# Chunked attention, Fourier mixing and an MLP on one core: the first batch's Fourier stage in halves, key blocks on partitions 32 to 127, and zero products in the planned gaps of TensorE

## The chip, the cores and the metric

The kernel runs on one core of a Trainium2 chip. The metric is the device time of one execution in microseconds (us). The engines are TensorE (PE; PEld is its weight load), VectorE (DVE), ScalarE (ACT), GpSimd (POOL) and SyncE (SP, which here only issues transfers).

## The reference

q, k and v are 4 batches x 8 heads x 768 positions x 64. Positions go in chunks of 32. Each chunk attends to 8 memory keys, the 16 positions before it, its own 32 and the 8 after it, with a softmax. The result, as x of 768 x 512 for each batch, goes through a two-dimensional Fourier transform of which the real part is kept, a norm, and an MLP of 512 to 2048 to 512:

```
X = fft(fft(x, axis=1), axis=2)
u = x + real(X)
un = (u - mean(u)) / sqrt(var(u) + 1e-6)
out = u + max(un @ w_ch1, 0) @ w_ch2
```

## The kernel before

**Planner.** `Plan` (L37 to L110) holds tasks: an engine, a cost in us, a function that emits the instructions, the tasks it comes after, the buffers it takes and gives (`take`, `give`) and a rank. `order` (L56) plays the time forward: whenever an engine is free in the plan, the first task by rank whose inputs are done and whose buffers are free is placed. What it emits is the fixed order of each engine's instructions; on the chip an engine never passes a waiting instruction. Loads count as `moved` us on one shared wire plus a lag of 2.0. PE costs count double before 40 us (L89).

**Attention** (L567 to L597) works on 16 pairs of heads, four for each batch, in the order 0, 2, 1, 3. Pair n: SP issues q, k (L256) and v in seven pieces (L275 to L281). Both are cast to bf16 (L262; on DVE for the first batch, on POOL for the others). PE turns them (`trq` L289, `trk` L305), ACT copies them out as `qT` (L294) and as key blocks `kTb` (L315), and DVE puts the memory keys in (L310). A key block is 96 rows: memory 0 to 7, then 88 positions. For each half g of the positions PE makes the scores `sc` (L326, 12 products), ACT the exponentials `e` (L334, two instructions), PE the values `xa` (L350, 24 products), and DVE divides by the sum into `xsb` (L360, L361), which is called the norm below. The first batch's `xa` uses two buffers in turn (tags xa, mlp).

**Fourier stage** (L646 to L706), per batch: DVE folds the channels (`zy` L374), then the sequence (`pq` L381, L382), then the channels again (`ff` L390, L391), for par 0 and 1. Each fold is split into two fp16 parts, `hi` on ACT (L399) and `lo` on DVE (L404). PE multiplies by the sequence tables (`ps` L414: 12 products for each of four parts, and 12 more for a single row). ACT and DVE copy the result out in two parts (`up` L426, L430) and DVE reverses it (`dn` L435). Then six blocks kt of columns follow: PE `pm` (L446), DVE sum and statistics (L452, L458, L459), ACT `un` (L464); the first batch's blocks are turned by PE (`tp` L471) and copied by DVE (`unT` L481), the others' by a transfer (L476). The sine tables are made on ACT after the first batch's last exponential (L617 to L622, L634). The weights are loaded through POOL's queue from the same point on (L640, L642).

**MLP** (L710 to L737), per batch in two halves of three blocks: 16 x 4 products `ph` (L497), ReLU on ACT to `hT` (L504, one buffer), 3 x 16 products `pc` (L511), DVE `osb` (L517) and the store (L521). Its tasks have the rank MLPS + number, so they are placed wherever nothing else is ready: they fill. This holds for the ReLU on ACT too:

```
def RELU(i):
    return MLPS + i
```

## Time and profile before

| | us |
|---|---|
| median of 3 runs (337.01 to 339.83) | 337.48 |
| the profiled execution's own time | 336.54 |
| its span | 334.8 |
| PE busy, of the span | 289.2 (86%) |
| DVE busy | 177.3 (53%) |
| ACT busy | 164.6 (49%) |
| POOL busy | 48.9 (15%) |
| PE `ph` L497, 512 products | 92.1 |
| PE `pc` L511, 384 products | 85.8 |
| chain that ended last: share of PE, DVE, ACT, DMA | 68%, 16%, 7%, 4% |

How to read it: 1.7 us of the execution's time lie outside the span. In a timeline each row is start, length, engine, line, operation, destination<-sources and count; square brackets give the engine's idle time before it and what ended that. The granted clock (PEclk) is 1.00 at 2.4 GHz and 0.50 at 1.2 GHz. The rows below read 1.00 up to 57 us as well, where the products take about twice as long as later.

### The profile page before, as it was taken

How to read it: one execution, taken by the hardware profiler on the slowest of the kernel's cores; microseconds unless marked ns; L12 is line 12 of the kernel's file. 1: busy time of each engine (PE TensorE's matmuls, PEld its weight loads, DVE VectorE, ACT ScalarE, POOL GpSimd, SP SyncE). 2: the span in 40 equal slices, each digit the busy share in tenths (PEclk: the TensorE clock that was granted, in tenths of full speed). 3: DMA queues.
4: the chain of work that ended last, by engine and by line, in shares of the span. 5: the costliest groups of instructions: out<-in, count | busy, mean ns of one | idle time of the engine just before them, and what ended most of it. 6: DMA issues, size and time to landing. Idle time of an engine off the chain costs nothing.

```text
span 334.8 us, 6729 instructions
## 1 busy us (share of the span) xinstructions
PE 289.2 (86%) x2761; PEld 187.1 (56%) x2761; DVE 177.3 (53%) x341; ACT 164.6 (49%) x290; POOL 48.9 (15%) x66
## 2 busy tenths in 40 slices
PE   0585847798999997978999996889999999999995
PEld 0464746676666674656745654655455454554542
DVE  5944169988599894998923369790110200101001
ACT  1364488556796546758525623246345062250620
POOL 8201471013333024320001000000010000000000
PEclk9999999899999999979999999799999999999999
DMA  8999899994999196980054200100420100101001
GB/s 168 208 217 197 180 226 205 198 216 118 206 184 162 55 224 129 232 139 3 2 113 117 29 2 2 40 23 33 108 80 2 63 32 31 65 2 63 31 33 63
DMA packets 60287, 35.18 MB, mean 105 GB/s; under 512 B 48480, under 2 KB 50528, under 8 KB 60256
## 3 DMA queue, kind: packets, MB, share of 16 engines
q1 hardware_dynamic: 53824, 24.19, 38.8%
q0 software_dynamic: 2688, 4.19, 6.9%
q10 hardware_dynamic: 3744, 6.36, 5.1%
q8 instruction: 22, 0.36, 0.5%
q14 instruction: 9, 0.07, 0.1%
HBM read 30.28 MB, written 6.29 MB: 109 GB/s over the span
## 4 chain that ended last, share of the span: by engine, by line
PE 68%; DVE 16%; ACT 7%; DMA 4%; issue 1%; SPq 1%; POOL 0%; ACTq 0%; POOLq 0%; DVEq 0%
PE pc L511 24%; PE ph L497 22%; PE xa L350 7%; PE ps L414 6%; PE pm L446 4%; ACT e L334 3%; PE sc L326 2%; DVE ff L391 2%; DVE lo L404 2%; DVE zy L374 2%; DMA mkf<-in_mem_k_dram 1%; DMA qf<-in_q_dram 1%; DMA unT<-un 1%; DVE xsb L361 1%; DVE pq L381 1%
## 5 line engine op out<-in xcount | busy, mean ns | idle before, releaser
L497 PE MATMUL ph<-unT,w_sb 128*128 128x384 f16 x512 | 92.1, 326 | 1.7 <-ACT hT L504 1.2
L504 ACT ACTIVATE hT<-ph 128x384 f16<-128x384 f32 x128 | 60.9, 490 | 65.2 <-PE ph L497 65.1
L511 PE MATMUL pc<-w_sb,hT 128*128 128x512 f16 x384 | 85.8, 379 | 0.0
L517 DVE SCALAR_TENSOR_TENSOR osb<-pc,rstd,xsb 128x512 f32<-128x512 f32 x24 | 18.0, 749 | 101.7 <-PE pc L511 101.7
L497 PEld LDWEIGHTS <-w_sb 128*128 128x128 f16 x512 | 48.1, 97 | 35.1 <-issue 6.2
L511 PEld LDWEIGHTS <-hT 128*128 128x128 f16 x384 | 37.2, 98 | 42.6 <-issue 0.3
L334 ACT ACTIVATE e<-sc,mbias 96x384 f32<-96x384 f32 x64 | 33.4, 571 | 22.2 <-PE sc L326 21.5
L350 PE MATMUL xa<-va,e 96*64 96x65 f32 x768 | 35.3, 252 | 10.2 <-ACT e L334 9.4
L350 PEld LDWEIGHTS xa<-va,e 96*64 96x64 f32 x768 | 30.4, 162 | 17.4 <-ACT e L334 10.4
L464 ACT ACTIVATE un<-xsb,mu_s 128x512 f16<-128x512 f32 x24 | 17.3, 720 | 29.1 <-DVE mu_s L459 9.1
L262 POOL CAST qb<-qf 96x1024 bf16<-96x1024 f32 x12 | 14.2, 1184 | 82.1 <-DMA qf<-in_q_dram 82.1
L360 DVE RECIPROCAL zs<-xa 128x6 f32<-128x6 f32 x32 | 6.1, 192 | 31.2 <-PE xa L350 31.1
L414 PE MATMUL ps<-cosS,hi 128*128 128x193 f16 (+1 forms) x72 | 16.6, 282 | 4.8 <-DVE ff L391 3.2
L414 PE MATMUL ps<-cosS,lo 128*128 128x193 f16 (+1 forms) x72 | 16.4, 282 | 4.8 <-DVE lo L404 4.8
L326 PE MATMUL sc<-qT,kTb 64*96 64x64 bf16 x384 | 16.9, 228 | 3.8 <-ACT kTb L315 2.0
L426 ACT CAST up<-ps 128x386 f16<-128x386 f32 x16 | 9.6, 603 | 18.7 <-PE ps L414 18.6
L326 PEld LDWEIGHTS <-kTb 64*96 64x96 bf16 x384 | 13.2, 141 | 9.8 <-issue 4.7
L361 DVE TENSOR_TENSOR xsb<-xa,zs 128x384 f32<-128x384 f32 x32 | 17.8, 557 | 1.1
L315 ACT COPY kTb<-trk 128x1056 bf16<-128x1056 bf16 x16 | 16.6, 1036 | 3.7 <-PE trk L305 3.7
L374 DVE TENSOR_TENSOR zy<-xsb 128x768 f32<-128x768 f32 x16 | 17.4, 1098 | 0.3
L414 PEld LDWEIGHTS <-lo 128*128 128x128 f16 (+1 forms) x120 | 13.3, 110 | 7.2 <-DVE lo L404 6.4
L452 DVE TENSOR_TENSOR xsb<-pm,xsb 128x512 f32<-128x512 f32 x24 | 16.0, 667 | 2.2 <-PE pm L446 2.2
(86 smaller groups left out, 316.0 us busy)
## 6 DMA issues: line engine op xcount, KB each, us to landing
va<-in_v_dram SPq DMA_DIRECT2D x32, 220.0 KB
qf<-in_q_dram SPq DMA_DIRECT2D x16, 384.0 KB
kf<-in_k_dram SPq DMA_DIRECT2D x16, 384.0 KB
out_dram<-osb ACTq DMA_DIRECT2D x24, 256.0 KB
w_sb<-in_moe_w_ch_dram POOLq DMA_DIRECT2D x8, 512.0 KB, 15.8
va<-in_mem_v_dram SPq DMA_DIRECT2D x32, 24.0 KB
va<-in_v_dram SPq DMA_DIRECT2D x32, 22.0 KB
va<-in_v_dram SPq DMA_DIRECT2D x16, 32.0 KB
```

What stands on the lines that cost most here:

```text
L315: nc.scalar.copy(strided(kTb[n % NKT], NMEM, [[WIN, NT], [RB, 11], [1, RB]]), strided(tr_of.pop((n, 1)), 0, [[64 // RB, NT], [1, 11], [KP, ...
L326: nc.tensor.matmul(sc[0:WIN, hh, t6, :], kT[r0:r0 + 64, t, :], qT[r0:r0 + 64, ts(t, 64)], start=True, stop=True, tile_position=(r0, 0))
L334: nc.scalar.activation(e1[:, :, :, ts(half, 32)], sc[0:WIN, :, 0:6, ts(half, 32)], AFT.Exp, bias=mbias[0:WIN, half:half + 1], scale=1.0 / ...
L350: nc.tensor.matmul(xa[64 * half:64 * half + 64, st, hh, 0:65], e1[:, hh, t6, :], v1[:, hh, 6 * g + t6, 0:65], start=True, stop=True)
L361: nc.vector.tensor_tensor(xs[b][:, 3 * g:3 * g + 3, 2 * pr * D:(2 * pr + 2) * D] .rearrange("p s (h d) -> p s h d", h=2), xa[:, :, :, 0:D] ...
L374: nc.vector.tensor_tensor(zy_of[b, par][:, :, c0:c0 + P], xb[:, :, c0:c0 + P], xb[:, :, HD + c0:HD + c0 + P], ALU.add if par == 0 else ALU ...
L414: nc.tensor.matmul(out_[:, sp, :], part[:, ab, sp * 3 + st, c0:c1], tab[:, sp, st, :], start=(st == 0 and i == 0), stop=(st == 2 and i == 1))
L464: nc.scalar.activation(un, xs[b][:, kt, :], AFT.Identity, bias=mu_of[b][:, kt, 0:1], scale=-1.0)
L497: nc.tensor.matmul(ph[:, 0:384], w1_sb[:, dt, ts(ht, P)], unT_of[b][:, dt, sh * 384:(sh + 1) * 384], start=(dt == 0), stop=(dt == NDT - 1))
L504: nc.scalar.activation(hT_of[b, sh][:, ht, :], ph_of.pop((b, sh, ht))[:, 0:384], AFT.Relu, bias=0.0, scale=-1.0)
L511: nc.tensor.matmul(pc_of[b, sh, stl], hT_of[b, sh][:, ht, ts(stl, P)], w2_sb[:, ht, :], start=(ht == 0), stop=(ht == NHT - 1))
L517: nc.vector.scalar_tensor_tensor(osb, pc_of.pop((b, sh, stl)), rstd_of[b][:, st:st + 1], xs[b][:, st, :], ALU.mult, ALU.add)
```

## The change

- **First Fourier stage in halves.** `first_fourier` replaces `fourier(0)`. The sequence fold `pq` is gone: the halves g (blocks 0 to 2, 3 to 5) are multiplied one after the other into the same PSUM buffer, the second half with negated tables `odd` for odd rows. That is 24 products for each of four parts and 24 for the single row, 120 where there were 60. The channel fold is made in two passes: the first (`pre`) needs head pairs 0 to 2 in plan order, the second the last pair. The middle column goes through the small tile `mid`.
- **Tables earlier.** The angles come first on DVE and the sines ahead of the attention's ACT tasks. `nsinD`, the negated tables and the table rows are made by POOL.
- **First batch's attention.** All casts go to POOL; DVE copies the key blocks of pairs 1 to 3; `xa` has one buffer.
- **Key blocks on partitions 32 to 127.** Memory keys start at 32, rows 0 to 31 are zero, and all of 128 are used in scores, exponentials and values. The zero rows around the keys are put in by the turn matrix `turn_b` and a fixed `kb` instead of by memsets of `kf`.
- **Weights** are loaded once the last v of the first batch is there (`e_gate`), in place of after its last exponential.
- **Planner.** Until PE's task after the norm of (3, 0) is placed, each gap of PE in the plan gets products of a zero tile (128 x 384, counted 0.17 us). PE costs double only before 7 us. After 45 us a PE task that is no filler (not MLP) may be placed 0.7 us before its inputs are done. ReLU, `osb` and stores have the first rank in place of the last. `tp` uses the tag mlp.

```diff
@@ -19,8 +19,8 @@
 RIGHT = 8
 NMEM = 8
 BIGM = 800.0
-OWN = NMEM + LEFT
-WIN = OWN + 64 + RIGHT
+MEM0 = 32
+OWN = MEM0 + NMEM + LEFT
...
     LAG = {"PE": 0.2, "DMA": 2.0}
+    FIRST = 45.0
+    WARM = 7.0
+    SLACK = 0.7
+    FILL = 0.17
+    filling, fill = None, None
...
+                    slack = (self.SLACK if e == "PE" and now > self.FIRST and not t["filler"]
+                             else 0.0)
-                    if any(a["done"] is None or a["end" if a["engine"] == e else "done"] > now
+                    if any(a["done"] is None
+                           or (a["end"] > now if a["engine"] == e else a["done"] > now - slack)
                            for a in t["after"]):
-                    cost = t["cost"] * (2.0 if e == "PE" and now < 40.0 else 1.0)
+                    cost = t["cost"] * (2.0 if e == "PE" and now < self.WARM else 1.0)
-                        t["done"] = t["end"] = wire + self.LAG["DMA"]
+                        t["done"] = t["end"] = wire + self.LAG["DMA"] + t["late"]
...
+                else:
+                    if e == "PE" and self.filling and self.filling[0]["at"] is not None \
+                            and self.filling[1]["at"] is None:
+                        cost = self.FILL * (2.0 if now < self.WARM else 1.0)
+                        idle[e] = now + cost
+                        placed.append(dict(engine="PE", cost=cost, emit=self.fill, at=now,
+                                           done=now + cost))
+                        moved = True
...
+    def g_zy(par, g):
+        if g == 0:
+            zy_of[0, par] = fpool.tile([P, NST, P], FP32, tag="unT", bufs=2, name="zy0")
+        xb, sl = xs[0], slice(3 * g, 3 * g + 3)
+        nc.vector.tensor_tensor(zy_of[0, par][:, sl], xb[:, sl, 0:P], xb[:, sl, HD:HD + P],
+                                ALU.add if par == 0 else ALU.subtract)
+
+    def g_ff(par, ab, g, last):
+        if (ab, g, last) == (0, 0, 0):
+            ff_of[0, par] = fpool.tile([P, 2, NST, P], FP32, tag="fold", bufs=2, name="ff0")
+        xb, sl = xs[0][:, 3 * g:3 * g + 3], slice(3 * g, 3 * g + 3)
+        zy, ff = zy_of[0, par][:, sl], ff_of[0, par][:, ab, sl]
+        plus = ab == par
+        if last:
+            plus = plus == (par == 0)
+        if not last:
+            if ab == 0:
+                nc.vector.tensor_copy(ff[:, :, 0], zy[:, :, 0])
+            elif par == 0:
+                nc.vector.memset(ff[:, :, 0:1], 0.0)
+        elif (par, ab) == (1, 1):
+            nc.vector.tensor_tensor(ff[:, :, 0], xb[:, :, P], xb[:, :, HD + P], ALU.subtract)
+        nc.vector.tensor_tensor(ff[:, :, 1:P], (ff if last else zy)[:, :, 1:P],
+                                rev_ap(xb, 2 * P - 1 + HD * last, P - 1, [[DM, 3]]),
+                                ALU.add if plus else ALU.subtract)
+
...
+    def g_rows(par, ab, g):
+        if g == 0:
+            ps_of[0, par, ab] = fps.tile([P, 2, NK], FP32, tag="acc" if par == 0 else "mlp",
+                                         name="ps")
+        ps = ps_of[0, par, ab]
+
+        todo = []
+        for sp in range(2):
+            tab = odd[:, ab] if g == 1 and sp == 1 else (cosS, sinS)[ab][:, sp]
+            one = odd[:, 0] if g == 1 and sp == 1 else cosS[:, sp]
+            part = [(ps[:, sp, :], g_hl(par, i)[:, ab, 3 * g + st, :], tab[:, st, :])
+                    for st in range(3) for i in range(2)]
+            if (par, ab) == (0, 1):
+                part[5:5] = [(ps[0:1, sp, :], mid[:, i, 3 * g + st, :], one[:, st, :])
+                             for st in range(3) for i in range(2)]
+            todo += part
+        for m, (out_, data, tab) in enumerate(todo):
+            nc.tensor.matmul(out_, data, tab, start=(g == 0 and m == 0),
+                             stop=(g == 1 and m == len(todo) - 1))
 
...
+    dz = cpool.tile([P, P], BF16)
+    fill_of = []
+    t_dz = add("DVE", 0.15, lambda: nc.vector.memset(dz, 0.0), rank=-30)
+
+    def e_fill():
+        if not fill_of:
+            fill_of.append(fps.tile([P, 512], FP32, tag="mlp", name="idle"))
+        nc.tensor.matmul(fill_of[0][:, 0:384], dz, strided(dz, 0, [[0, 3], [1, P]]),
+                         start=True, stop=True)
+
+    t_fill = add("PE", 0.33, e_fill, [t_dz], take=("mlp",), rank=-1)
+    plan.fill = e_fill
...
+    ANG = dict(S=-18, D=-10)
...
-                      take=(("qf", "kf")[i],), moved=1.2) for i in range(2)]
+                      take=(("qf", "kf")[i],), moved=1.3, late=0.0 if b == 0 else 3.0)
+                  for i in range(2)]
         lv = add("SP", 2.8, lambda: e_load_v(n), [t_ones[n] if n < NV else None],
-                 take=("va",), moved=2.6)
-        ce, cn, cc = (nc.vector, "DVE", 0.68) if first else (nc.gpsimd, "POOL", 1.04)
-        cq, ck = [add(cn, cc, lambda i=i, e=e: e_cast(n, i, ce), [e], take=(("qb", "kb")[i],),
+        cq, ck = [add("POOL", 1.1, lambda i=i, e=e: e_cast(n, i, nc.gpsimd), [e],
+                      rank=11 + 0.1 * n + 0.01 * i if b == 0 else None, take=(("qb", "kb")[i],),
                       give=(("qf", "kf")[i],)) for i, e in enumerate((lq, lk))]
+        dve = ("DVE", nc.vector.tensor_copy) if 0 < n < HP else ("ACT", None)
-        tk = add("PE", 0.43, lambda: e_turn_k(n), [ck, t_idb], take=(ktag,), give=("kb",))
-        mk = add("DVE", 0.2, lambda: e_mkT(n), [t_mkT], take=("kTb",))
-        ek = add("ACT", 1.0, lambda: e_kT(n), [tk, mk], give=(ktag,))
+        tk = add("PE", 0.43, lambda: e_turn_k(n), [ck, t_idb, t_kz], take=(ktag,), give=("kb",))
+        mk = t_mk[n] = add("DVE", 0.2, lambda: e_mkT(n), [t_mkT, t_kTz[n % NKT], t_mk.get(n - 1)],
+                           take=("kTb",))
+        ek = add(dve[0], 1.0, lambda: e_kT(n, dve[1]), [tk, mk], give=(ktag,))
...
-            tag = "mlp" if first and g == 1 else "xa"
+            tag = "xa"
             v_ = add("PE", 0.85, lambda g=g: e_values(n, g), [x_, lv], take=(tag,),
+                     rank=len(plan.tasks) + (50 if (n, g) == (2, 1) else 25) if first else None,
...
+    def e_negatives():
+        for i, tab in enumerate((cosS, sinS)):
+            nc.gpsimd.tensor_scalar(odd[:, i], tab[:, 1], -1.0, None, ALU.mult)
...
-    t_sines = add("ACT", 6.2, e_all_sines, [t_angle["S"], t_angle["D"], x_last])
-    t_rows = add("DVE", 1.3, e_table_rows, [t_sines])
+    t_sines = add("ACT", 6.9, e_all_sines, [t_angle["S"], t_angle["D"]], rank=SINES)
+    t_neg = add("POOL", 1.4, e_negatives, [t_sines], rank=100)
+    t_rows = add("POOL", 1.8, e_table_rows, [t_sines, t_neg], rank=101)
+    def e_gate():
+        nc.gpsimd.tensor_copy(gate[64:65], va[(HP - 1) % NV][64:65, 1, NT - 1, 0:1])
+
+    t_gate = add("POOL", 0.1, e_gate, [t_lv[HP - 1]])
     t_w2 = [add("POOL", 0.7, lambda g=g: nc.gpsimd.dma_start(
-        w2_sb[:, ts(g, 4), :], w2v[:, ts(g, 4), :]), [x_last], moved=3.5) for g in range(4)]
+        w2_sb[:, ts(g, 4), :], w2v[:, ts(g, 4), :]), [t_gate], moved=3.0) for g in range(4)]
...
+    def first_fourier():
+        t_rest, t_mid, pre = {}, {}, {}
+        plan.filling = (t_fill, add("PE", 0.0, lambda: None, [t_norm[HP - 1, 0]], give=("mlp",)))
+        for g in range(2):
+            for par in range(2):
+                zy = add("DVE", 0.5, lambda par=par, g=g: g_zy(par, g),
+                         [t_norm[0, g], t_norm[1, g], t_sines],
+                         take=("unT",) if g == 0 else ())
+                for ab in range(2):
+                    pre[par, ab, g] = add("DVE", 0.62,
+                                          lambda par=par, ab=ab, g=g: g_ff(par, ab, g, 0),
+                                          [zy, t_norm[2, g]],
+                                          take=("fold",) if (ab, g) == (0, 0) else (),
+                                          give=("unT",) if (ab, g) == (1, 1) else ())
+        for g in range(2):
+            t_mid[g] = add("DVE", 0.4, lambda g=g: g_mid(g), [t_norm[2, g], t_norm[3, g]],
+                           rank=len(plan.tasks) + 8)
+            for par in range(2):
+                for ab in range(2):
+                    end = (ab, g) == (1, 1)
+                    ff = add("DVE", 0.5 + 0.1 * par * ab,
+                             lambda par=par, ab=ab, g=g: g_ff(par, ab, g, 1),
+                             [pre[par, ab, g], t_norm[3, g]])
+                    hi = add("ACT", 0.5, lambda par=par, ab=ab, g=g: g_hi(par, ab, g), [ff],
+                             take=(("hl",), ("hT",))[par] if (ab, g) == (0, 0) else ())
+                    lo = add("DVE", 0.48, lambda par=par, ab=ab, g=g: g_lo(par, ab, g), [hi],
+                             give=("fold",) if end else ())
+                    tag = ("acc", "mlp")[par]
+                    rw = add("PE", 2.0 if (par, ab) == (0, 1) else 1.0,
+                             lambda par=par, ab=ab, g=g: g_rows(par, ab, g),
+                             [lo, t_mid[g], t_neg], take=(tag,) if g == 0 else (),
+                             give=(("hl",), ("hT",))[par] if end else ())
+                    if g == 1:
+                        up = add("ACT", 0.6, lambda par=par, ab=ab: e_up(0, par, ab), [rw],
+                                 take=("up",))
+                        t_rest[par, ab] = add("DVE", 0.6,
+                                              lambda par=par, ab=ab: e_rest(0, par, ab), [up],
+                                              give=(tag,))
+        return columns_of(0, t_rest)
...
-            tp = add("PE", 0.26, lambda kt=kt: e_turn_u(b, kt), [un, t_idh], take=("acc",),
+            tp = add("PE", 0.26, lambda kt=kt: e_turn_u(b, kt), [un, t_idh], take=("mlp",),
                      give=("un",))
             t_un[kt] = add("DVE", 0.43, lambda kt=kt: e_unT(b, kt), [tp, t_un.get(kt - 1)],
-                           take=("unT",) if kt == 0 else (), give=("acc",))
+                           take=("unT",) if kt == 0 else (), give=("mlp",))
...
-                         rank=MLPS + len(plan.tasks))
+                         rank=MLPS + len(plan.tasks), filler=True)
...
-                          rank=MLPS + len(plan.tasks))
+                          rank=RELU(len(plan.tasks)))
     def RELU(i):
-        return MLPS + i
-    done = {0: fourier(0)}
+        return i - MLPS
+
+    done = {0: first_fourier()}
```

## Rows read from the trace of the kernel before

**Rows 1.** Busy by stretch: span, length, PE, PEld, DVE, ACT, POOL, PEclk, DMA, GB/s

```profile
0.00:46.65 46.65, 27.15 (x389) 22.96 (x389) 23.93 (x62) 20.58 (x30) 17.87 (x38) 1.00 1.04 196
46.65:57.00 10.35, 4.85 (x56) 4.23 (x56) 9.88 (x19) 9.40 (x15) 3.40 (x3) 1.00 1.07 221
57.00:78.72 21.72, 17.58 (x234) 14.62 (x233) 19.56 (x43) 12.66 (x22) 1.04 (x1) 0.92 1.15 211
78.72:226.23 147.51, 135.39 (x1541) 92.08 (x1539) 112.16 (x204) 83.10 (x146) 25.03 (x23) 0.98 0.49 96
226.23:330.85 104.62, 104.20 (x548) 53.25 (x547) 11.06 (x15) 38.83 (x80) 1.59 (x2) 1.00 0.14 46
```

**Rows 2.** Timeline: the first batch's last norm, its first columns, the first MLP products

```profile
46.09 0.56 DVE L361 TENSOR_TENSOR xsb<-xa,zs 128x384 f32<-128x384 f32 x1
...
68.06 0.39 PE L446 MATMUL pm<-cosD,up 128*128 128x256 f16 x2
...
78.72 0.81 PE L497 MATMUL ph<-unT,w_sb 128*128 128x384 f16 x4
```

**Rows 3.** Timeline of PE: values of pair 4 behind the sine tables

```profile
52.15 1.57 PE L350 MATMUL xa<-va,e 96*64 96x65 f32 x24 [5.73 <-ACT e L334]
```

**Rows 4.** Timeline: pair 0 from its k cast to its second norm; pair 3's k

```profile
9.36 1.45 DVE L262 CAST kb<-kf 100x1024 bf16<-100x1024 f32 x1
...
19.92 0.56 DVE L361 TENSOR_TENSOR xsb<-xa,zs 128x384 f32<-128x384 f32 x1
...
27.03 0.69 DVE L262 CAST kb<-kf 100x1024 bf16<-100x1024 f32 x1 [1.02 <-DMA kf<-in_k_dram]
```

**Rows 5.** Timeline of SP: the last pieces of pair 3's v

```profile
24.26 2.52 SPq L271 DMA_DIRECT2D va<-in_v_dram  x2
```

**Rows 6.** Timeline of PE at the full clock: turns, scores, MLP, values

```profile
87.93 0.46 PE L326 MATMUL sc<-qT,kTb 64*96 64x64 bf16 x12
88.32 0.82 PE L497 MATMUL ph<-unT,w_sb 128*128 128x384 f16 x4
89.07 0.92 PE L350 MATMUL xa<-va,e 96*64 96x65 f32 x24
89.92 0.53 PE L305 MATMUL trk<-ident_b,kb 100*128 100x100 bf16 x8
90.29 0.81 PE L497 MATMUL ph<-unT,w_sb 128*128 128x384 f16 x4
```

**Rows 7.** DVE by line, 46.65 to 79 us: busy us, mean ns, idle before

```profile
L404 DVE TENSOR_TENSOR lo<-ff,hi 128x768 f16<-128x768 f32 x4 | 4.2, 1040 | 0.4 <-ACT hi L399 0.4
...
L391 DVE TENSOR_TENSOR ff<-pq 128x762 f32<-128x762 f32 x4 | 3.8, 940 | 0.0
```

**Rows 8.** Timeline of DVE: the first stage's last split

```profile
63.67 0.94 DVE L404 TENSOR_TENSOR lo<-ff,hi 128x768 f16<-128x768 f32 x1
```

**Rows 9.** Timeline: two POOL casts and the DVE fold beside them

```profile
82.96 1.03 POOL L262 CAST qb<-qf 96x1024 bf16<-96x1024 f32 x1
83.94 1.04 POOL L262 CAST kb<-kf 100x1024 bf16<-100x1024 f32 x1
...
83.20 2.59 DVE L374 TENSOR_TENSOR zy<-xsb 128x768 f32<-128x768 f32 x1
```

**Rows 10.** PE by line, 0 to 79 us: busy us, mean ns, idle before

```profile
L350 PE MATMUL xa<-va,e 96*64 96x65 f32 x264 | 16.0, 302 | 9.9 <-ACT e L334 9.4 <-issue 0.5
L326 PE MATMUL sc<-qT,kTb 64*96 64x64 bf16 x168 | 8.7, 251 | 1.3 <-ACT kTb L315 1.3
L289 PE MATMUL trq<-ident_b,qb 96*128 96x96 bf16 x64 | 6.0, 260 | 4.7 <-POOL qb L262 2.6 <-DVE qb L262 2.1
L305 PE MATMUL trk<-ident_b,kb 100*128 100x100 bf16 x56 | 5.6, 273 | 1.6 <-DVE kb L262 1.6
```

**Rows 11.** Waits of PE, 80 to 330 us: total us, times, longest

```profile
PE ps L414 <- DVE lo L404: 4.6, 5, 2.4
...
PE ph L497 <- ACT hT L504: 1.2, 2, 0.6
```

**Rows 12.** Chain of waits, in order of time: a half batch of MLP

```profile
278.84 10.36 PE pc L511 x48
289.20 10.40 PE ph L497 x64
```

More of the change, by code (lines that the diff above doesn't have):

```diff
@@ L48, in add @@
     def add(self, engine, cost, emit, after=(), take=(), give=(), rank=None, moved=0.0,
-            loose=False):
+            loose=False, late=0.0, filler=False):
         t = dict(engine=engine, cost=cost, emit=emit, after=[a for a in after if a is not None],
                  take=take, give=give, rank=len(self.tasks) if rank is None else rank,
-                 moved=moved, done=None, at=None, no=len(self.tasks), loose=loose)
+                 moved=moved, done=None, at=None, no=len(self.tasks), loose=loose,
+                 late=late, filler=filler)
         self.tasks.append(t)
@@ L367 @@
     zy_of, pq_of, ff_of, hl_of, ps_of, up_of, pm_of, un_of, tp_of = ({} for _ in range(9))
-    mu_of, unT_of, rstd_of = {}, {}, {}
+    mu_of, unT_of, rstd_of, g_of = {}, {}, {}, {}
+    mid = cpool.tile([P, 2, NST, 1], FP16)
+    mid32 = cpool.tile([P, NST, 1], FP32)
+    gate = cpool.tile([P, 1], FP32)
     def e_zy(b, par, c):
@@ new lines, in g_hl, with g_hi @@
+    def g_hl(par, which):
+        if (par, 0) not in g_of:
+            if par == 0:
+                g_of[0, 0] = fpool.tile([P, 2, NST, P], FP16, tag="hi", bufs=1, name="hi0")
+                g_of[0, 1] = fpool.tile([P, 2, NST, P], FP16, tag="lo", bufs=1, name="lo0")
+            else:
+                both = fpool.tile([P, 2, 2, NST, P], FP16, tag="hT", bufs=1, name="hl1")
+                g_of[1, 0], g_of[1, 1] = both[:, 0], both[:, 1]
+        return g_of[par, which]
+    def g_hi(par, ab, g):
+        sl = slice(3 * g, 3 * g + 3)
+        nc.scalar.copy(g_hl(par, 0)[:, ab, sl], ff_of[0, par][:, ab, sl])
@@ L684, in columns @@
                            allr + [t_rows] + (list(t_dn.values()) if kt > 2 else []),
-                           take=("acc",),
+                           take=("acc",), rank=len(plan.tasks) + (15 if kt == 3 else 0),
                            give=("up",) * 4 if kt == 2 else ("dn",) * 4 if kt == 5 else ())
@@ L729, in mlp @@
                              give=("hT",) if stl == 2 and end else (),
-                             rank=MLPS + len(plan.tasks))
+                             rank=MLPS + len(plan.tasks), filler=True)
                 os_ = add("DVE", 0.76, lambda sh=sh, stl=stl: e_osb(b, sh, stl), [c2, rs],
```

147 lines of the change are left out of this document (84 added, 63 removed).

## The prediction, made before the changed kernel was run

> **What bounds the kernel now.** I read the busy time by stretch first [rows 1]. From the first MLP products at 78.72 us [rows 2] to the end of the products at 330.85 us TensorE is short of work for 12.1 us (147.51 - 135.39) and 0.4 us (104.62 - 104.20); one MLP half, 16 x 4 and 48 products, runs as 10.40 and 10.36 us without a hole [rows 12]. Before 78.72 us it is idle for 29 us (19.5 + 5.5 + 4.1), and most of what it does there runs at half pace: 24 value products take 1.57 us in the front [rows 3] and 0.85 us, start to start, at 89 us [rows 6]. The granted clock reads 1.00 for both, so in the front the durations are the better witness: they belong to the lower level, 1.2 GHz. So the end is set by when the MLP filler first becomes available, plus the TensorE work that is then left, plus its holes. The timeline gives three marks for the first part: the first batch's last norm ends at 46.65 us, its first columns run at 68.06, the first MLP products at 78.72 [rows 2]. That is 46.7 + 21.4 + 10.7 us.
>
> The transfers are saturated through all of the front: share 1.04 to 1.15, about 200 GB/s [rows 1]. No edit loads fewer bytes, so the loads put a floor under the first mark.
>
> **The change, step by step.** All sums are made against the profiled execution's 336.54 us; the median of the runs shown is 0.94 us higher.
>
> *The last norm.* The sines leave their place between pair 3 and pair 4 (the 5.73 us hole of [rows 3] is that block) and run on ACT from about 10 us, where ACT waits for the first turns anyway; pair 0 is then some 6 us late, which the floor of the loads hides. Its floor: k of pair 3 is there at 27.03 us [rows 4]; the last pieces of its v are issued from 24.26 to 26.8 us [rows 5]. From k to the second norm pair 0 takes 11.1 us (9.36 to 20.48, [rows 4]) with TensorE at half pace. If the zero products hold the upper level, the two value groups save 2 x 0.72, the scores and the turn about 1 more: 8.7, and 27.03 + 8.7 = 35.7. The single `xa` buffer makes each value group wait for the norm of the one before, and the cast on POOL takes 1.04 instead of 0.69 [rows 9, 4]; pair 0's two groups were also apart by more than that, so I add 0.3: **36**, 10.6 us earlier. Bounds: 33, if the handovers overlap better, and 42, if TensorE stays slow and pair 0's lateness is handed on through the `va` buffer which pair 3's loads need.
>
> *Last norm to columns.* The first-pass folds, about 15 us of DVE with norms and key copies, lie in the 20 us from 14 to 34 in which DVE waits for loads; if that cover is gone they come on top. After the norm of (3, 0) at about 34.5 remain, on DVE: 8 last folds and 8 splits of half size (0.94 and 0.94 for the whole ones [rows 7, 8], so 0.5 each: 8.0), the middle column 2 x 0.4 and a third operand column twice 0.1, and the second norm 0.76: 9.8, to 44.3. The tail behind the last split is 3.45 us now (64.61 to 68.06, [rows 2, 8]) with 24 products at the lower level; with 12 at the upper one I take 2.4: 46.7. The 60 additional row products are 5 us at the upper level; all but the last group lie beside DVE's list. Added: POOL now has work beside this list, the casts of pairs 4 and 5. A fold which takes about 0.95 took 2.59 us beside two POOL casts [rows 9]: it began 1.78 us before the second cast's end at 84.98 and ended 0.81 us behind it. Four casts in this list could so cost 0 to 4.2 us; I take the middle, 2.1, since the gate and the weight loads' issue on POOL push some of them out. **48.8** for the first columns, 12.8 us behind the last norm instead of 21.4.
>
> The Trainium skill, "SBUF — State Buffer", section "Who interferes with whom", goes further: a VectorE instruction with two SBUF inputs and a GpSimd one that reads SBUF exclude one another for a whole instruction. This fold agrees with it to 0.1 us; by that rule all four casts would be paid and the sum would be 2.1 us higher, about 324.
>
> *Columns to MLP.* 10.7 us now. The first MLP half needs three of six blocks, and `tp` no longer competes with the columns for `acc`. Between the present 10.7 and half of it, I take 8.5, nearer to the present: **57.3** for the first MLP products. That is 21.4 earlier. The weights are issued some 10 us earlier too; they stay off the path unless they land after 57.
>
> *What is left then.* By 79 us TensorE had done 11 value groups (264 products by 24), 14 score groups, 8 and 7 turns [rows 10], so beyond the first batch 3, 6, 4 and 3. At the upper level (0.85, 0.39 and about 0.4, [rows 6]) that is 2.6 + 2.3 + 2.8 = 7.7 us. By 57 us the loads allow pair 4 and the turns and first scores of pair 5: 2 x 0.85 + 3 x 0.39 + 4 x 0.4 = 4.5. So **+3.2** of work goes behind the mark.
>
> *Wider key blocks.* 128 weight columns for 96 in 26 score groups that are left. They may be hidden behind the products; if the loads set the pace, 0.39 grows by a third, 26 x 0.13 = 3.4. Transposes with 128-column loads run at 0.046 us each [rows 6], which would make it 12 x 0.046 = 0.55: 4.2. A gain is not excluded (1). I take **+1**. Exponentials and values keep their free sizes: nothing.
>
> *Waits that the planner now allows.* A task that is not MLP may be put on TensorE 0.7 us early; what it waits, nothing fills, and the MLP behind it waits too. There are 12 pairs x 5 such tasks (two turns, first scores, two value groups) and 3 x 5 (four rows, the first columns): 75. No row shows it; bounds are nothing, and 75 x 0.25 = 19 us. Many will be ready already, because TensorE was busy with another task of the same kind. I take **+4**, near the lower end because all waits behind 80 us now sum to about 12 [rows 1, 11].
>
> *ReLU first.* TensorE waited 1.2 us for ReLU [rows 11]; I take **-1**. `osb` and stores had slack.
>
> Sum: 336.5 - 21.4 + 3.2 + 1 + 4 - 1 = 322.3; **322 us**. The other holes behind the mark I leave as they are; the later batches' stages are the same code.
>
> **Rivals.** *(a) The zero products do not hold the clock.* They are planned against loads that arrive several us late, and a long wait could drop TensorE again. For it: the front at half pace though TensorE is over half busy [rows 1]. Against: it is the gaps that go. Price: 2.5 us on the last norm, and the second half's 60 products at half pace, 9.6 us against DVE's 4.6 us, about 3 more: 327.5. *(b) The loads take it back.* The front moves, but batch 1's q, k and v come no earlier, as the queues are full to 79 us. From 57 us there are 41.5 us of batch 0's MLP [rows 12] and some 35 us of attention and Fourier work to bridge until batch 1's columns are turned, and each in-order wait for a late cast goes into the end. At 12 us of such holes the time is 334. *(c) Slower: the early placement.* If each of the 75 tasks waits 0.35 us, the mean of an even spread from 0 to 0.7, that is 26 us, 22 more than in the sum: 344. It decides from 0.31 us a task on (23 us, 341). Against it: casts and exponentials are planned longer than they run, so inputs come before their planned time. *(d) Better:* with the filler there from 57 us, the 12.1 us of holes shrink by half, the casts cost nothing and the front reaches 54: 322 - 6 - 2 - 3 = 311, and less with a last norm at 33.
>
> **How the numbers follow.** My forecast, 322 with its own range of 312 to 331, gets 0.62; (a) 0.12; (b) 0.10; (c) 0.06; (d) below 312, 0.10. The range has the front's bounds (54 to 63), 0 to 10 us of planner waits and -1 to 3.4 for the score loads: 307 to 336, which leaves (c), a part of (b) and the best of (d) out. About 1% is what runs of this kernel can tell from no change: below 334.1 is faster, above 340.9 slower. Forecast, (a), (d) and half of (b) are faster: 0.88; the other half of (b) and a little of (c) 0.07; slower 0.05.
>
> **What would show it.** Last norm near 36, first columns near 49, first MLP products near 57 us; value groups at 0.85 us from about 10 us on; TensorE's holes behind the mark between 10 and 18 us in sum; DVE folds stretched beside POOL casts. I am wrong if the first MLP products come after 66 us, or if the holes behind them grow by more than the mark has gained.

## The result and the profile after

The changed kernel takes **316.54 us** (median of 4 runs, 316.42 to 317.28) beside 337.39 for the kernel before on the same chip: ratio 0.937, 95% interval 0.933 to 0.942. The forecast was 322. The profiled execution has a span of 315.5 us against 334.8.

Busy time by stretch, after: start and end, length, then busy us (instructions) of PE, PEld, DVE, ACT, POOL, the granted clock, the DMA share and GB/s. The marks are those of [rows 1, 2].

```profile
0.00:44.63 44.63, 38.26 (x487) 24.56 (x487) 31.00 (x75) 19.71 (x30) 34.63 (x58) 0.92 0.93 181
44.63:62.73 18.10, 14.72 (x152) 11.93 (x153) 13.91 (x35) 8.53 (x16) 2.06 (x2) 0.81 1.15 217
62.73:71.97 9.24, 8.71 (x134) 7.44 (x129) 8.07 (x18) 5.24 (x9) 1.03 (x1) 1.00 1.03 200
71.97:226.00 154.03, 152.13 (x1726) 99.58 (x1724) 112.94 (x214) 96.04 (x172) 26.58 (x25) 1.00 0.53 116
226.00:311.58 85.58, 85.16 (x451) 43.68 (x448) 9.01 (x12) 30.30 (x64) 1.59 (x2) 1.00 0.10 37
```

The span fell by 19.3 us, but not where the forecast put it. The first MLP products come 6.8 us earlier (78.72 to 71.97), not 21.4. The stretch from there to the last product is 12.5 us shorter (252.1 to 239.6): TensorE's holes in it went from 12.5 to 2.3 us, and its busy time from 239.6 to 237.3.

Timeline of the front, after:

```profile
14.87 1.39 DVE L332 COPY kTb<-mkT 128x96 bf16<-128x96 bf16 x2
15.57 3.48 PE L644 MATMUL idle<-dz 128*128 128x384 bf16 x11
19.25 2.93 PE L644 MATMUL idle<-dz 128*128 128x384 bf16 x17
22.94 0.35 PE L348 MATMUL sc<-qT,kTb 64*128 64x64 bf16 x12
26.05 0.92 PE L369 MATMUL xa<-va,e 128*64 128x65 f32 x24
27.25 0.56 DVE L380 TENSOR_TENSOR xsb<-xa,zs 128x384 f32<-128x384 f32 x1
...
41.11 1.03 POOL L285 CAST qb<-qf 96x1024 bf16<-96x1024 f32 x1
41.31 1.24 DVE L482 TENSOR_TENSOR ff<-zy,xsb 128x381 f32<-128x381 f32 x1
42.48 1.00 DVE L477 COPY ff<-zy 128x3 f32<-128x3 f32 x1
44.07 0.56 DVE L380 TENSOR_TENSOR xsb<-xa,zs 128x384 f32<-128x384 f32 x1
47.49 0.34 PE L530 MATMUL ps<-cosS,lo 128*128 128x193 f16 x1 [0.99 <-DVE lo L502]
62.73 0.39 PE L541 MATMUL pm<-cosD,up 128*128 128x256 f16 x2
71.97 0.82 PE L592 MATMUL ph<-unT,w_sb 128*128 128x384 f16 x4
101.67 0.35 PE L348 MATMUL sc<-qT,kTb 64*128 64x64 bf16 x12
101.95 1.04 PE L606 MATMUL pc<-w_sb,hT 128*128 128x512 f16 x4
```

The key blocks of pair 0 are complete at 16.26, but zero products and turns of the next pair stand ahead of its scores until 22.94. From the first norm (27.25) to the last (44.07) the eight groups follow one another at 1.9 to 3.2 us. Then 119 row products run back to back from 47.49 to 60.87.

Waits of PE behind 72 us, after; all the waits of the Fourier rows in [rows 11] are gone:

```profile
PE ph L592 <- ACT hT L599: 0.9, 4, 0.3
PE ph L592 <- DVE osb L612: 0.6, 3, 0.2
PE sc L348 <- ACT e L356: 0.5, 1, 0.5
```

### The profile page after: what moved, and what is told of

Read it like the earlier page. It is cut to its first block, busy times and chain, and to the rows that moved or that the text cites. A ratio compares the mean times of both kernels' runs of the same rounds, so it can differ in the third digit from the quotient of the medians.

```text
span 315.5 us, 7131 instructions
## 1 busy us (share of the span) xinstructions
PE 299.0 (95%) x2939; PEld 187.2 (59%) x2939; DVE 175.7 (56%) x353; ACT 159.8 (51%) x289; POOL 65.9 (21%) x88
## 4 chain that ended last, share of the span: by engine, by line
PE 83%; DVE 10%; ACT 4%; issue 2%; DMA 1%; POOL 0%; POOLq 0%; ACTq 0%
PE ph L592 25%; PE pc L606 24%; PE xa L369 8%; PE pm L541 6%; PE ps L436 5%; PE ps L530 4%; PE idle L644 4%; PE sc L348 3%; PE trq L312 2%; PE trk L327 2%; ACT e L356 1%; DVE osb L612 1%; DVE xsb L380 1%; DMA out_dram<-osb 1%; DVE ff L482 1%
## 5 line engine op out<-in xcount | busy, mean ns | idle before, releaser
L356 ACT ACTIVATE e<-sc,mbias 128x384 f32<-128x384 f32 x64 | 33.7, 579 | 10.3 <-PE sc L348 7.9
L285 POOL CAST qb<-qf 96x1024 bf16<-96x1024 f32 x16 | 17.8, 1114 | 66.4 <-DMA qf<-in_q_dram 47.0
L369 PEld LDWEIGHTS xa<-va,e 128*64 128x64 f32 x768 | 25.0, 137 | 8.0 <-issue 6.4
L369 PE MATMUL xa<-va,e 128*64 128x65 f32 x768 | 29.4, 226 | 0.1
L644 PE MATMUL idle<-dz 128*128 128x384 bf16 x118 | 25.7, 371 | 1.0 <-DVE dz L639 1.0
L317 ACT COPY qT<-trq 128x768 bf16<-128x768 bf16 x16 | 12.8, 799 | 16.6 <-PE trq L312 16.6
L281 POOL CAST kb<-kf 96x1024 bf16<-96x1024 f32 x16 | 17.9, 1117 | 10.4 <-PE trk L327 8.4
L448 ACT CAST up<-ps 128x386 f16<-128x386 f32 x16 | 9.7, 604 | 16.8 <-PE ps L436 9.3
L644 PEld LDWEIGHTS <-dz 128*128 128x128 bf16 x118 | 12.1, 110 | 10.1 <-issue 4.2
L553 DVE BATCH_NORM_STATS2 st<-xsb 128x6 f32<-128x512 f32 x24 | 16.4, 683 | 0.5
L337 ACT COPY kTb<-trk 128x1056 bf16<-128x1056 bf16 x13 | 13.5, 1038 | 3.9 <-PE trk L327 3.9
```

Of the source, the lines that this page charges most:

```text
L281: eng.tensor_copy(kb[0:QP].rearrange("p j h d -> p h j d"), src[n % NS].rearrange("p h (j d) -> p h j d", j=RB))
L285: eng.tensor_copy(of[n].rearrange("p j h d -> p h j d"), src[n % NS].rearrange("p h (j d) -> p h j d", j=RB))
L356: nc.scalar.activation(e1[:, :, :, ts(half, 32)], sc[:, :, 0:6, ts(half, 32)], AFT.Exp, bias=mbias[:, half:half + 1], scale=1.0 / math.sqr ...
L369: nc.tensor.matmul(xa[64 * half:64 * half + 64, st, hh, 0:65], e1[:, hh, t6, :], v1[:, hh, 6 * g + t6, 0:65], start=True, stop=True)
L644: nc.tensor.matmul(fill_of[0][:, 0:384], dz, strided(dz, 0, [[0, 3], [1, P]]), start=True, stop=True)
```

## The experiments

All times are medians; the ratio is to the kernel before, run on the same chip. Marks and stretches are of the profiled execution: end of the last norm, first columns, first MLP products, the stretch from there to the last product, and TensorE's idle time in it (length less busy).

| kernel | us | ratio, 95% | norm | columns | MLP | stretch | holes |
|---|---|---|---|---|---|---|---|
| before | 337.4 | | 46.65 | 68.06 | 78.72 | 252.1 | 12.5 |
| changed | 316.5 | 0.933 to 0.942 | 44.63 | 62.73 | 71.97 | 239.6 | 2.3 |
| e1 no zero products | 316.9 | 0.937 to 0.945 | 43.28 | 62.1 | 71.35 | 239.7 | 2.6 |
| e2 no early placement | 322.1 | 0.952 to 0.961 | 44.03 | 59.9 | 70.03 | 246.3 | 6.9 |
| e3 ReLU, `osb` last | 329.2 | 0.971 to 0.983 | 43.25 | 61.6 | 70.8 | 252.4 | 10.4 |
| e4 96-row key blocks | 316.2 | 0.930 to 0.941 | 43.54 | 61.8 | 71.0 | 241.6 | 2.2 |
| e5 first Fourier whole | 325.6 | 0.960 to 0.971 | 42.66 | 68.9 | 77.6 | 242.2 | 5.4 |
| e6b before + ReLU first | 329.1 | 0.970 to 0.980 | 46.16 | 68.0 | 78.7 | 243.6 | 6.9 |
| e6 e6b + early placement | 325.1 | 0.959 to 0.970 | 46.83 | 70.8 | 81.2 | 236.5 | 2.4 |
| e12 early costs measured, no zeros | 318.9 | 0.941 to 0.949 | 45.41 | 63.5 | 73.5 | 240.0 | 3.1 |
| e13 the same with zeros | 315.8 | 0.929 to 0.941 | 43.42 | 60.9 | 71.1 | 238.7 | 2.2 |
| e7 sines planned shorter | 315.4 | 0.928 to 0.939 | 44.08 | 60.7 | 69.9 | 239.8 | 2.5 |
| e15 early placement from 62 | 314.7 | 0.924 to 0.938 | 43.44 | 57.95 | 68.3 | 240.6 | 3.5 |
| e17 e7 + e15 + zeros longer | 314.1 | 0.923 to 0.930 | 43.41 | 57.3 | 67.5 | 242.0 | 3.7 |

Up to the last norm the changed kernel, e2, e3 and e15 have the same order of instructions on TensorE, DVE, ACT and POOL, and yet this norm ends between 43.25 and 44.63 us. A difference of up to 1.4 us in this mark, and in what follows from it, is therefore one of executions and not of kernels.

### Zero products out

```diff
-                    if e == "PE" and self.filling and self.filling[0]["at"] is not None \
-                            and self.filling[1]["at"] is None:
+                    if False:
```

> The changed kernel without the zero products; all else as it was. Theory 1, the zero products hold the upper clock level through the first batch and are worth it: without them the value groups before 45 us take 1.57 us again, the first row products run at 0.16 us each, the first MLP products come 2 to 6 us after 72 us, and the time is 318 to 323. Rival, they pad: 32 of them stand between the first turns and the first scores, which start at 22.9 us although their key block is complete at 16.3; without them the first scores come at about 16 to 17 us, the first MLP products at 66 to 70 us and the time is 311 to 315 in spite of a slower clock.

316.87: no difference. Timeline of e1:

```profile
19.70 0.50 PE L347 MATMUL sc<-qT,kTb 64*128 64x64 bf16 x12
23.46 1.57 PE L368 MATMUL xa<-va,e 128*64 128x65 f32 x24
32.45 0.92 PE L368 MATMUL xa<-va,e 128*64 128x65 f32 x24 [0.24 <-DVE xsb L379]
```

Without zero products the first scores come 3.2 us earlier; in return the first groups run at half pace, and the level rises only near 31 us. In this order the two cancel.

### Early placement out, and ReLU last again

```diff
-    SLACK = 0.7
+    SLACK = 0.0
```

> The changed kernel with the 0.7 us of early placement set to 0. Theory of the prediction, early placement costs TensorE waits (4 us, bounds 0 to 19): the holes behind the first MLP products stay near 2 us or shrink, and the time is 312 to 316. Rival, early placement is one of the things that closed the holes of before (12.5 us behind the mark there, 2.3 us in the changed kernel): the holes come back by 3 to 8 us and the time is 319 to 325.

322.11, 5.6 us slower: the prediction's sign was wrong. The first MLP products come 1.9 us earlier without it, of which 0.6 is there already at the last norm. The stretch behind is 6.7 us longer: 4.6 in holes, of which one wait is 4.4 us, and 2.1 in TensorE's busy time. The longest wait of PE behind 70 us, e2:

```profile
PE trq L312 <- POOL qb L285: 4.4, 1, 4.4
```

```diff
     def RELU(i):
-        return i - MLPS
+        return MLPS + i
```

> The changed kernel with ReLU, output sums and stores at the last rank again, as in the kernel before. Theory, ReLU and output first is what keeps the filler ready and closed the holes (2.3 us behind the mark against 12.5 in the kernel before): without it 5 to 10 us of holes come back, with one or two half-clock stretches, and the time is 322 to 328. Rival, the order of these tasks is worth the 1.2 us that the prediction read from the waits for ReLU: 317 to 318.

329.2, 12.7 us slower, and none of it in the front. The stretch behind the mark is 12.8 us longer: 8.1 in holes, which are 10.4 us now, and 4.7 in TensorE's busy time, which holds two stretches of 3.4 us at a granted clock of 0.50. ReLU is named for 1.0 of the holes. Waits of PE behind 70.8 us, e3:

```profile
PE ps L436 <- DVE lo L426: 2.6, 3, 1.5
PE ph L592 <- ACT hT L599: 1.0, 3, 0.5
```

### The planner's two edits on the kernel before

e6 has both, e6b the rank alone:

```diff
     def RELU(i):
-        return MLPS + i
+        return i - MLPS
...
+                    slack = (self.SLACK if e == "PE" and now > self.FIRST and not t["filler"]
+                             else 0.0)
```

> The kernel before with two edits of the planner alone: a TensorE task that is not MLP may be placed 0.7 us early after 45 us, and ReLU, output sums and stores come first. Front, key blocks, casts and first Fourier stage as before. Theory, the order closed the holes: 5 to 13 us of the 16 us of holes and half-clock stretches behind the first MLP products go, and the time is 324 to 332. Rival, the holes closed because the first batch's stage and the loads were moved: 335 to 338, no change.

> The kernel before with one edit alone: ReLUs, output sums and stores ranked ahead of all else on their engines. Early placement (0.7 us before an input is ready) is not in it. Theory (the two planner edits add up): with both the kernel before fell from 337.3 to 325.1, and taking early placement out of the changed kernel cost 5.5, so 325.1 + 5.5 = 330 to 331 us, with waits of the Fourier rows (ps behind lo and ff, 7.8 us before) gone for the larger part. Rival (rank does all of it, early placement is worth something only where the front is shorter): 325 to 326. Second rival, the prediction's -1 for the rank: 336.

e6b 329.11, e6 325.11: of 20.9 us the rank alone gives some 8, early placement 4 more, and all the rest of the change (halves, tables, key blocks, zero products) the last 8.6. So the edits do not add up singly: taken out of the changed kernel, the rank costs 12.7 and early placement 5.6.

Early placement's share hangs on one wait in each pair of runs. e2 has the one of 4.4 us above, and e6b one of nearly the same size; the changed kernel and e6 have neither:

```profile
PE sc L333 <- ACT e L341: 4.0, 1, 4.0
```

Both go back to transfers. In e2 POOL's cast had waited 9.47 us for a load of q; in e6b ACT stood for 6.10 us before a transfer of `unT` let it go on. Kernels that place early have such waits too (8.01 us in e5, 1.9 in e17). So the 4 to 5.6 us are measured, but whether early placement keeps such waits away, or these two orders happened upon one, is not shown.

What the rank does is seen in the kernel before. Its largest hole is a wait that [rows 11] leaves out:

```profile
PE ps L414 <- DVE ff L391: 3.2, 1, 3.2
```

The timeline around it:

```profile
196.20 7.07 PE L511 MATMUL pc<-w_sb,hT 128*128 128x512 f16 x32
209.63 0.26 PE L414 MATMUL ps<-cosS,hi 128*128 128x193 f16 x1 [3.24 <-DVE ff L391]
210.76 0.37 PE L414 MATMUL ps<-cosS,hi 128*128 128x193 f16 x1
211.89 0.74 DVE L517 SCALAR_TENSOR_TENSOR osb<-pc,rstd,xsb 128x512 f32<-128x512 f32 x1
215.84 0.74 DVE L517 SCALAR_TENSOR_TENSOR osb<-pc,rstd,xsb 128x512 f32<-128x512 f32 x1
```

The same stretch of e6b:

```profile
201.64 0.74 DVE L524 SCALAR_TENSOR_TENSOR osb<-pc,rstd,xsb 128x512 f32<-128x512 f32 x1
208.96 2.20 PE L504 MATMUL ph<-unT,w_sb 128*128 128x384 f16 x12 [0.33 <-DVE osb L524]
```

Before, two blocks of 16 `pc` products were done by 203.3, and their `osb`, ranked behind all Fourier folds on DVE, ran at 211.89 and 215.84. Until then both PSUM buffers of the tag mlp were held and no MLP product could be placed: TensorE stood before the next Fourier row, and the wait bears that row's name. With the rank turned `osb` comes at once and MLP products fill the stretch. And TensorE, which had rested there, no longer goes on at the lower level (0.37 us for a row product at 210.76; 0.25 in e6b at 212.76).

The second largest hole, 2.4 us up to 144.49 [rows 11], is not one of `osb`. There both buffers were held by MLP products that were done at 141.7 and whose ReLU, at the last rank as well, ran 2.6 and 4.4 us later on ACT. Timeline of the kernel before:

```profile
140.20 1.47 PE L497 MATMUL ph<-unT,w_sb 128*128 128x384 f16 x8
144.24 0.50 ACT L504 ACTIVATE hT<-ph 128x384 f16<-128x384 f32 x1
146.08 0.49 ACT L504 ACTIVATE hT<-ph 128x384 f16<-128x384 f32 x1
```

The edit turns ReLU, `osb` and the stores together; what each is worth by itself was not measured.

### Key blocks back on 96 rows

```diff
-MEM0 = 32
+MEM0 = 0
+WIN = 96
```

> The changed kernel with its key blocks back on partitions 0 to 95, so the weights of the score products are 96 columns wide and the zeroing of 32 rows of each v buffer (three of 1.4 us on POOL) is gone. Theory (the width of the weights is what made the scores faster): twelve score products take 0.39 us start to start again, as before, and not 0.28; 32 groups, 26 of them behind the first MLP products, cost 0.11 x 26 = 2.9 us more, so 319 to 320 us. Rival (the scores became faster through their place in the order, and the width costs or gives nothing): the groups stay at 0.28 and the time at 316 to 317. Second rival, the prediction's own +1 for wider blocks: 315.5, a gain of 1.

316.16: no difference in the time, and yet the theory on the width is right. Timeline of e4, against the last two rows of the changed kernel's timeline above:

```profile
101.47 0.46 PE L346 MATMUL sc<-qT,kTb 64*96 64x64 bf16 x12
101.86 1.04 PE L604 MATMUL pc<-w_sb,hT 128*128 128x512 f16 x4
```

Twelve score products take 0.39 us start to start with 96 columns of weights and 0.28 with 128, at the same place. The weight loads alone are shorter too. By line, the changed kernel and then e4 (the mean is the number behind the busy time, in ns):

```profile
L348 PEld LDWEIGHTS <-kTb 64*128 64x128 bf16 x384 | 7.6, 95 | 9.3 <-issue 7.9 <-DVE zy L464 0.3 <-ACT hT L599 0.2
L346 PEld LDWEIGHTS <-kTb 64*96 64x96 bf16 x384 | 11.4, 120 | 9.0 <-issue 7.6 <-DVE zs L377 0.3 <-ACT hT L597 0.2
```

TensorE is busy 2.1 us longer behind the mark with 96 rows; 21 score groups at 0.11 us are 2.3. Why the time does not show it is open. e4 need not zero 32 rows of each v buffer (1.4 us each on POOL, ahead of pair 1's casts), and its first MLP products come 0.9 us earlier, but executions of one order differ by as much. Its four runs spread from 314.85 to 318.35 us, and the profiled one is the slowest of them.

### The first Fourier stage whole

```diff
-    done = {0: first_fourier()}
+    plan.filling = (t_fill, add("PE", 0.0, lambda: None, [t_norm[HP - 1, 0]], give=("mlp",)))
+    done = {0: fourier(0)}
```

> The changed kernel with the first batch's Fourier stage whole, as the other batches have it. Theory (the halves shorten the way from the last norm to the columns): it is 21.4 us again as in the kernel before, and not 18.1, the first MLP products come 3.3 us later, at about 75, and the time is 319 to 321 us. Rival (TensorE fills that way with the second batch's attention, which has to be done at some time anyway, so the halves bring nothing): the first MLP products come 3 us later or more, but the stretch behind them is shorter by as much, and the time is 316 to 317.

325.62, 9.1 us slower, more than either view said. Timeline of e5:

```profile
47.47 0.96 DVE L426 TENSOR_TENSOR lo<-ff,hi 128x768 f16<-128x768 f32 x1
53.16 0.82 PE L312 MATMUL trq<-ident_b,qb 96*128 96x96 bf16 x8 [8.01 <-POOL qb L285]
53.78 0.36 PE L436 MATMUL ps<-cosS,hi 128*128 128x193 f16 x1
```

The columns come 26.2 us behind the norm (42.66), 18.1 in halves. But the halves are only a part of these 8.1 us. The first operand of the rows was there at 48.4; in TensorE's order a turn of pair 5 stood ahead of them and waited for POOL's cast, which had waited 9.96 us for its load. That is 5.3 us, and the first rows then ran at the lower level (0.37). What remains, about 3 us, is the size that the first theory gave for the halves, but the rows at the lower level are in it, and the two were not taken apart. The stretch behind the mark is 2.6 us longer as well, with another wait of this kind (2.8 us).

### Why the last norm does not move

e12 takes the zero products out and gives the planner the early costs of the trace; e13 is e12 with zero products; e7 alters the sines' cost alone.

```diff
-    t_sines = add("ACT", 6.9, e_all_sines, [t_angle["S"], t_angle["D"]], rank=SINES)
+    t_sines = add("ACT", 4.6, e_all_sines, [t_angle["S"], t_angle["D"]], rank=SINES)
```

```diff
-        t_ones[i] = add("POOL", 0.5, lambda i=i: e_edge_ones(i), [e_], rank=14)
+        t_ones[i] = add("POOL", 1.9, lambda i=i: e_edge_ones(i), [e_], rank=14)
...
-    t_neg = add("POOL", 1.4, e_negatives, [t_sines], rank=100)
+    t_neg = add("POOL", 3.4, e_negatives, [t_sines, t_cast[HP - 1]], rank=100)
```

> The changed kernel without its zero products, with the planner's costs for the early work as the trace has them (sines 4.6 us and not 6.9, edge rows of v 1.9 and not 0.5, zeroed key blocks 1.4 and not 0.8, identity copies 1.6 and not 0.6, negated tables 3.4 and 2.8 and not 1.4 and 1.8) and the negated tables behind pair 3's casts. So pair 0's scores stand ahead of pair 1's key turn, which waited for POOL until 18.3. Theory (the front is late because the plan put pair 0 late, and that was handed on through the v buffer to pair 3): first scores at 16 to 17.5 us and not 19.7 (or 22.9), pair 3's v landed at 31 to 32 and not 33.8 (35.1), last norm at 41 to 42 and not 44.6, time 312.5 to 314.5 us. Rival (the loads set the last norm: the DMA engines are busy at over 0.9 up to 45 us whatever is done): first scores earlier, last norm at 43.5 to 45, time 316 to 317.

> The kernel with the planner's early costs as measured, now with the zero products in TensorE's planned gaps again (115 of them). It differs by them alone from the run before. Theory (both matter: the plan's order sets when pair 0 starts, TensorE's pace how long the eight value groups take): value groups take 0.92 us instead of 1.57, first scores at 18.5 to 20 us, from the first values seven steps of 2.24 us as in the changed kernel, last norm at 40 to 41.5 us instead of 45.4, time 312 to 314 us. Rival 1 (zero products are planned at 0.17 us, run at 0.32 at the lower clock and push real work back as much as the clock gives): first scores at 21 to 23, last norm at 43.5 to 45, time 316 to 318. Rival 2 (loads or POOL set the last norm, TensorE's pace does nothing): last norm at 45, 318.5 to 319.5.

> The changed kernel with one number altered: the sine tables are planned at 4.6 us, as they run, and not 6.9, so the plan has pair 0's scores at 15.9 and not 18.1 us and 107 zero products instead of 118. Theory (pair 0 is late because of the plan, and the lateness goes through to the last norm): first scores at 20 to 21 us and not 22.9, last norm at 42 to 43, time 314 to 315.5. Rival (the last norm hangs on something else): 316 to 317, whatever the first scores do.

318.94, 315.8 and 315.4; e12 and e13 lie outside the ranges of their theories. Busy time by stretch (columns as above), e12 first, then the same stretches of e13:

```profile
32.00:36.00 4.00, 3.14 (x52) 2.93 (x51) 3.91 (x8) 2.21 (x5) 3.94 (x4) 0.57 1.24 206
36.00:40.00 4.00, 2.35 (x40) 1.91 (x38) 3.96 (x11) 1.50 (x3) 3.94 (x14) 0.50 0.89 202
```

```profile
32.00:36.00 4.00, 3.21 (x64) 2.23 (x63) 3.94 (x7) 1.74 (x3) 3.94 (x8) 1.00 1.03 219
36.00:40.00 4.00, 4.00 (x83) 2.82 (x81) 3.97 (x12) 1.79 (x4) 3.94 (x10) 1.00 0.78 197
```

The pair isolates the zero products: they keep the upper level from 32 to 40 us and are worth 3.1 us in this order. e7's time is in the range of its theory, but not by its way: its last norm stays at 44.1, and its rows run at a clock of 0.82 from 48 to 52 us, where the changed kernel's run at 0.50 (this level can differ between executions of one order, see e15 below). The theory that pair 0's start sets the last norm falls. First scores were at 18.7, 19.9, 20.9 and 22.9 us in e12, e13, e7 and the changed kernel, the last norm at 45.4, 43.4, 44.1 and 44.6. In e13 the first norms come 3 us earlier than in the changed kernel, but the fifth, pair 2's first, ends 3.9 us behind the fourth. Timeline of e13 there:

```profile
31.74 2.82 DVE L464 TENSOR_TENSOR zy<-xsb 128x384 f32<-128x384 f32 x3
35.13 0.56 DVE L380 TENSOR_TENSOR xsb<-xa,zs 128x384 f32<-128x384 f32 x1
35.60 1.25 DVE L337 COPY kTb<-trk 128x1056 bf16<-128x1056 bf16 x1
36.96 0.35 PE L348 MATMUL sc<-qT,kTb 64*128 64x64 bf16 x12
```

DVE is busy for 3.9 of 4 us there (the third pair of numbers behind the length): first-pass folds, norms and key copies share it. The fifth norm's values were done at 33.93 us, but three folds held DVE until 34.56, and pair 3's scores wait for its key copy. So at an earlier start DVE's list is the next limit: from the first norm's end to the last one's it is 18.6 us in e13, 16.8 in the changed kernel. Whether the loads or the single buffers come right behind it was not settled.

### Early placement later, and a better version

e15 lets early placement begin behind the first batch's rows; e17 adds e7's edit and zero products up to the last norm.

```diff
-    FIRST = 45.0
+    FIRST = 62.0
```

```diff
-    plan.filling = (t_fill, add("PE", 0.0, lambda: None, [t_norm[HP - 1, 0]], give=("mlp",)))
+    plan.filling = (t_fill, add("PE", 0.0, lambda: None, [t_norm[HP - 1, 1]], give=("mlp",)))
```

> The changed kernel with early placement from planned 62 us on instead of 45, so behind the first batch's row products alone. Theory (placed early there, turns and scores of pairs 4 and 5 stand ahead of the columns and TensorE waits for them in order: last norm to columns took 18.1 us with it and 15.9 without): columns 2 us earlier, first MLP products at 70 us, holes behind them still 2 to 4 us, time 314 to 315.5 us. Rival (the work that stood ahead has to be done behind, and the second pair's start sets later waits): columns 2 us earlier, but the stretch behind the MLP's start longer by 2 us or more, 316 to 319.

> The changed kernel with three edits together: early placement from planned 62 us on, sine tables planned at 4.6 us, and zero products up to the last norm itself instead of the one before. Theory (gains of the two single edits, 1.1 and 1.8 us against 316.5, hold together, and the row products keep the upper clock level, 0.085 us a product instead of 0.16 at first): row products of the first batch in 11 us and not 13.4, first columns at 57 to 58.5 us, first MLP products at 67 to 68.5, time 312.5 to 314 us. Rival (both edits win the same microseconds, those of the row products at the lower clock level): 314.5 to 315.5.

314.71 and **314.06** (312.54 to 315.2). e17's ratio, 0.923 to 0.930, lies below the changed kernel's 0.933 to 0.942: it beats both. Busy time by stretch for the row products, the changed kernel first, then e17, then e15:

```profile
48.00:52.00 4.00, 4.00 (x25) 3.05 (x24) 3.93 (x12) 1.44 (x3) 0.00 (x0) 0.50 1.06 239
```

```profile
48.00:52.00 4.00, 4.00 (x47) 3.67 (x46) 3.93 (x13) 1.71 (x4) 0.00 (x0) 1.00 1.10 244
```

```profile
48.00:52.00 4.00, 4.00 (x46) 3.49 (x45) 3.93 (x13) 2.14 (x6) 0.00 (x0) 1.00 1.14 203
```

At the upper level 47 products fit into 4 us, at the lower 25. The columns of e17 come 5.4 us earlier and the MLP 4.4; 2.4 us of it are given back behind that, 1.4 of these as holes. That each of the three edits has a share is not shown: e15's interval holds e17's ratio (0.926) and overlaps the changed kernel's. And e15's rows ran at the upper level too (1.00), though its zero products end where those of the changed kernel do and the order up to the last norm is the same. So the level of the rows can differ between executions, and neither e15's columns, 4.8 us earlier where 2 were expected, nor e17's can be put down to their edits alone.

## Why the prediction was right or wrong

The time is inside the range and near the middle of the main case, but that case's own test, first MLP products before 66 us, failed: large errors of both signs offset one another. The front was to give 21.4 us and gave 6.8; the stretch behind it was to cost 7.2 us (3.2 + 1 + 4 - 1) and gave 12.5. That the sum came within 6 us is luck.

**The last norm: 36 expected, 44.63 measured; this step failed.** The words were "pair 0 is then some 6 us late, which the floor of the loads hides". Its first values came 11.3 us later (14.7 to 26.05), and pair 3 does not start when its keys land: it stands in order behind seven groups which take 2.4 us each from norm to norm, 16.8 us in sum. The bound of 42, given for a slow TensorE and a lateness handed on through the `va` buffer, was the better value and still too early; yet TensorE was not slow (1.00 from 20 us on), and pair 3's v was there at 35.13 us, 4.5 before its first values. The cover named for the first-pass folds failed with it: the DVE wait "from 14 to 34" passed before their inputs were there, and they ran from 32 to 45, among the norms.

**Last norm to columns: 12.8 expected, 18.1 measured.** The sum was made on DVE. DVE's list did end early (54.7 us), but the row products came as one dense block: 13.4 us of TensorE, 2.4 of them through the lower level (45.80 to 56.8 in e17, 11.0 us). Rival (a) had named a price for this stage, though for its second half, and it was the first. Its cause is another: the zero products do hold the clock (e12, e13), but they end ahead of the sparse stretch from 42.6 to 47.5 us, in which it drops here (in e15 it did not). The POOL casts cost about what was said, but 1.5 us of it at another place: a fold of 0.55 took 1.24 us and a copy of 0.16 took 1.00 beside two casts, so the last norm began 1.2 us after its values. The fold ended at 42.55, 0.41 us behind the cast (42.14). That agrees to 0.14 us with the rule of the Trainium skill, "SBUF — State Buffer", "Who interferes with whom", that the two exclude one another. Columns to MLP: 8.5 expected, 9.2 measured.

**The holes behind the mark, which "I leave as they are".** Holes of 10 to 18 us were expected, and 2.3 were left. Here the missing 10.2 us came from, and the failed term is *ReLU first*, **-1**, with "`osb` and stores had slack". It was read from the wait that bore ReLU's name, 1.2 us. The price was in the waits of the Fourier rows, 7.8 us (4.6 in [rows 11] and the 3.2 above): at the largest a late `osb` had taken the filler away, at the next a late ReLU. For the smaller ones the reason was not looked up. The rank alone is worth 8 us, in the changed kernel 12.7.

**Early placement: +4 expected; it gains 4 (on e6b) to 5.6 us (e2).** The bound from below was nothing; a gain was not considered. The changed kernel's PE waits behind the mark sum to 2.2 us over all tasks, so hardly one of the 75 waits at all, and rival (c) is out. Why it gains is open: in both comparisons a single wait that goes back to a transfer, 4.0 and 4.4 us, is the larger part.

**Wider key blocks: +1 expected; TensorE gains 2.1 us behind the mark**, though the time of e4 does not show it. A gain of 1 was one of the bounds and the better end; no row of before showed a score product with 128 columns. The Trainium skill, "TensorE: Matmul & The Clock Gate", "Weight-path perf modes — Fast Weight Load (FWL) and DoubleRow", says that a fast weight load applies at 128 weights of a type other than FP32. The step from 96 columns (0.39) to 128 (0.28) agrees with it, and so do the loads (120 and 95 ns).

**Work moved behind the mark: +3.2 expected and found:** 10 value groups, 11 score groups and 12 turns before it, against 11, 14 and 15 [rows 10], at the prices of the sum. But so much work was expected by 57 us, and by 72 no more was done; the agreement is luck.

**A term that was missing: half pace behind holes.** The 0.98 of [rows 1] over 147.5 us is some 6 us at the lower level, which cost 3 (an estimate); it went with the holes (1.00 after). With it TensorE's busy time behind the mark nearly closes: 3.2 more work, 2.1 less for scores, 3 less for the clock are 1.9 less, and 2.3 were measured.

## What to carry to other kernels

A wait in an order that a planner wrote names the next instruction, not the reason why nothing else was there; look for the filler that could not be placed, and for the small late task that held its buffer. When pairs run through single buffers in order, the last one stands behind all the steps before it, and its own data can land early in vain; an earlier start helps only as far as those steps do not lengthen. Rank what frees a buffer of the filler ahead of everything: here that was worth 8 us alone and 12.7 in the changed kernel. Before a difference between two marks is explained, see what the same order gives in another execution.

## What the runs showed of the hardware

Products of a zero tile raise and hold TensorE's clock as others do: in the changed kernel they take 0.32 us each from 15.57 us on and 0.17 from 19.25, before any score or value product has run, while in e1 the level rises only near 31 us. Twelve products with 128 weight columns are faster (0.28 us) than with 96 (0.39). And the granted clock of e1 reads 1.00 in a stretch whose value groups take 1.57 us: as in [rows 3], durations are the better witness there.
